# An attention-and-FFN kernel whose work order is written out, with the fourth pair's queries and keys issued ahead of four loads of values

## The chip, the cores and the metric

The kernel runs on one core of a Trainium2 chip. A core has five instruction streams: TensorE (PE, matrix multiplies into eight banks of PSUM), VectorE (DVE), ScalarE (ACT), GpSimd (POOL) and SyncE (SP). Each takes its instructions strictly in the order in which the program gave them to it. Data moves between HBM and the core's own memory (SBUF) by DMA; an engine issues a DMA as one more instruction of its stream. The metric is the device time of one execution in microseconds (us), median over the runs shown.

## The reference

The work is one block of attention and one gated feed-forward network. `q`, `k` and `v` are float32 of shape (8 batches, 8 heads, 576 positions, 64). For each of the 64 heads two attentions are added:

```python
q_d = q.reshape(B, H, Sd, 4, D).mean(axis=3)      # k_d, v_d alike; Sd = 144
out_d = softmax(scale * q_d @ k_d.T) @ v_d        # 144 x 144 scores
out_up = np.repeat(out_d, 4, axis=2)
mask = np.abs(pos[:, None] - pos[None, :]) < 4    # a band of 7 positions
out_local = softmax(where(mask, scale * q @ k.T, -1e9)) @ v
attn_out = out_up + out_local                     # (8, 8, 576, 64)
x = attn_out.transpose(0, 2, 1, 3).reshape(4608, 512)
out = (np.maximum(x @ w_gate, 0) * (x @ w_val)) @ w_out
```

`w_gate` and `w_val` are 512 x 1536, `w_out` is 1536 x 512, the output is 4608 x 512, all float32. The kernel computes in float16 and accumulates in float32.

## The kernel before, in words

**Tiling.** Heads are worked in pairs, 32 of them: pair p holds two heads of batch p // 4. The four pairs of a batch give the 512 columns of x for that batch's 576 tokens, pair kk of the batch giving the 128 columns of group kk (tile `xT`). The feed-forward network then runs on these tokens: for each of twelve blocks of 128 hidden columns a gate product and a value product (4 matmuls each, one for each kk), a ReLU on ACT, a product on DVE; after that the second product `y` with `w_out`, a copy on ACT and a store.

**Names.** An operation is named by its kind and its pair or its tokens. For pair p:

- `lq`, `lk` load queries and keys (SP, L1430); `lv0` to `lv3` load values in pieces (SP, L1674 and L1680; lv0 is an edge piece of two DMAs). SP keeps eight loads in flight: each waits for the landing of the one eight before.
- `cast` turns q and k into float16 (L1329 on ACT, L1330 on DVE or POOL), `T` transposes them on PE and sums the pooled groups (L1456, L1460), `ev0` and `ev1` copy the transposed halves out of PSUM, `pl` the pooled ones (both L1329/L1330).
- `Sl` and `Sd` are the local and the pooled scores on PE (L1518, L1530); for later pairs they stand together as `S`. `mx`, `sub`, `exp`, `sm`, `rc`, `nrm` are the local softmax: maximum (DVE, L1573), subtraction (L1576), exponential (ACT, L1589), sum (DVE, L1611), reciprocal (DVE, L1613), product (L1615). `dmx`, `nb`, `exd0..2`, `rcd`, `nrd` are the pooled one: maximum (DVE, L1592), its negative (POOL, L1595), exponentials (ACT, L1605), reciprocal (DVE, L1627), product (L1631).
- `tr0`, `tr1` transpose the local weights on DVE (L1621), `W` the pooled ones on PE, and `evw` copies the latter out.
- `vc` casts the values to float16 (`vw`), `VP` pools them on PE (L1695), `vd` copies that out (`vdz`).
- `V` multiplies weights with values on PE (L1731, L1739), `od` copies one half of its result on ACT (L1750), and `xa0`, `xa1` add the other half to it on DVE and write `xT` (L1759).
- `hg` and `hv` are the gate and value products of the feed-forward network (PE, L1798), `rl` the ReLU (ACT, L1812), `gm` the product (DVE, L1819). `hg0_0` is hidden block 0 of the first 512 tokens. Only for the blocks 0 and 1 the products are split: the part `a` takes the columns of pairs 0 to 2 and the part `b` those of pair 3. `hg512_0` and `hg512_6` take the last 64 tokens of the batch, six hidden blocks at once.
- `wg`, `wv` load three hidden blocks of the first weights each (POOL's DMA queue, L1380), `wo` the second ones.

**Stages.** The first four pairs are the *head* of the program: their q and k are loaded in another form (48 partitions, into the tile `gT`) and nothing of the feed-forward network can run until three pairs are done. From then on, attention of the next batch is worked between the products of the current one.

**What sets the order.** The kernel builds a graph of 1771 operations, each with its engine or a choice of engines, a length, a priority and what it depends on. A planner, `list_schedule` (L1071), simulates the five engines, the DMA engines and the fetch of instructions, and always takes the operation that can start first; ties go by priority. The tables `RANKS`, `SHIFT` and `ASK` move single operations in this. The planner also picks the engine of an operation that has a choice (`alts`), the PSUM banks, and how many matmuls on zeros PE runs in a gap ahead of an operation (`fill`, L1360). Operations are then emitted in the planned order of their starts, and that order is what each engine's stream holds:

```python
order = list_schedule(ops, {"F": [0, 1, 2, 3], "A": [4, 5, 6, 7]},
                      {PE: 0.05, ACT: 0.05, DVE: 0.05, POOL: 0.05, SP: 0.05})
```

The planner's numbers act on the order alone; at run time an engine starts an instruction when the one before it is done and what it waits for has arrived.

## Time and profile before

| | before |
|---|---|
| median of 3 runs | 362.51 us |
| lowest and highest | 362.36 and 363.07 us |
| profiled execution, device time | 361.35 us |
| its span, first to last instruction | 359.6 us |
| granted TensorE clock in it | 0.999 |

The profiled execution is 1.16 us (0.3%) under the median, so differences that are read from it are worked against 361.35 us and carried to the median afterwards. 1.75 us of it lie around the span.

The views used below are these. The *page* gives the busy time of each engine and the chain of work that ended last, by engine. The *windows view* gives one row for each stretch of time: the stretch and its length; for PE, weight loads (PEld), DVE, ACT and POOL the busy time with the number of instructions; the granted clock; the share of the DMA engines; GB/s. The *timeline* lists instructions by their start: start, length, engine, line, operation, output<-inputs, shape, and in brackets the idle time of the engine ahead of it with what ended it. The *groups view* puts instructions with one line, engine, operation and shape together: count, then busy us and the mean ns of one, then the idle time ahead of them. The *view of DMA issues* gives for one group of transfers its KB each and the median us from issue to landing.

### The profile page before, as it was taken

Reading aid. Unit: us, or ns where it says so; the run is one execution under the profiler, and the core shown is the slowest. Engines: PE = TensorE matmul, PEld = TensorE weight load, DVE = VectorE, ACT = ScalarE, POOL = GpSimd, SP = SyncE. Lnnn points to the kernel's source line nnn. Section 1 sums busy time; section 2 is a strip of 40 time slices with the busy share of each in tenths; the row PEclk is TensorE's granted clock in tenths of the full one; section 3 lists DMA queues with packets and bytes.
Section 4 is the critical chain, followed back from the end, with each engine's and each line's share of the span. In section 5 each row is a group of like instructions: output and inputs, shape, how many; then the busy total and the mean of one; then the engine's idle time right before and its main releaser. Section 6 shows DMA issues by size and latency. Waiting matters only on the chain.

```text
span 359.6 us, 10503 instructions
## 1 busy us (share of the span) xinstructions
PE 350.2 (97%) x4241; PEld 182.5 (51%) x4241; DVE 247.9 (69%) x477; ACT 202.8 (56%) x481; POOL 204.5 (57%) x240
## 2 busy tenths in 40 slices
...
GB/s 190 201 272 255 195 227 292 110 185 152 259 232 212 228 280 167 278 224 264 198 230 233 190 271 182 215 261 224 217 237 65 47 93 26 0 60 59 0 75 102
DMA packets 122067, 64.80 MB, mean 180 GB/s; under 512 B 100386, under 2 KB 106402, under 8 KB 122018
## 3 DMA queue, kind: packets, MB, share of 16 engines
...
q0 software_dynamic: 5824, 4.72, 8.6%
...
## 4 chain that ended last, share of the span: by engine, by line
PE 90%; POOL 5%; DMA 1%; issue 1%; DVE 1%; ACT 1%; POOLq 0%; SPq 0%
PE bank L1798 52%; PE bank L1864 25%; PE bank L1518 4%; PE bank L1731 2%; PE bank L1739 2%; DMA gT<-in_q_dram 1%; PE bank L1530 1%; POOL wo_sb L1330 1%; PE bank L1640 1%; PE bank L1695 1%; POOL vw L1352 1%; POOL wd L1631 1%; PE bank L1843 1%; POOL vw L1330 1%; POOL e L1615 1%
## 5 line engine op out<-in xcount | busy, mean ns | idle before, releaser
L1819 DVE TENSOR_TENSOR gT<-r,bank 128x512 f16<-128x512 f16 (+1 forms) x112 | 74.6, 666 | 64.1 <-PE bank L1798 59.9
L1798 PE MATMUL bank<-xT,wg_sb 128*128 128x512 f16 (+2 forms) x528 | 112.2, 341 | 0.0
L1798 PE MATMUL bank<-xT,wv_sb 128*128 128x512 f16 (+2 forms) x528 | 112.2, 341 | 0.0
L1812 ACT ACTIVATE r<-bank 128x512 f16<-128x512 f32 (+1 forms) x112 | 65.1, 583 | 67.2 <-PE bank L1798 62.9
L1864 PE MATMUL bank<-wo_sb,gT 128*128 128x512 f16 x420 | 96.6, 379 | 0.0
L1798 PEld LDWEIGHTS <-wg_sb 128*128 128x128 f16 x528 | 44.2, 98 | 45.5 <-issue 0.4
L1798 PEld LDWEIGHTS <-wv_sb 128*128 128x128 f16 x528 | 44.2, 98 | 44.6 <-issue 0.6
L1864 PEld LDWEIGHTS <-gT 128*128 128x128 f16 x420 | 39.8, 98 | 44.6 <-issue 0.4
L1873 ACT COPY y_sb<-bank 128x512 f32<-128x512 f32 x35 | 20.5, 586 | 52.0 <-PE bank L1864 49.6
L1330 POOL CAST vw<-vw 128x1536 f16<-128x1536 f32 x28 | 40.9, 1461 | 2.7 <-DMA vw<-in_v_dram 1.9
L1507 DVE TENSOR_REDUCE qkd<-qkT 128x288 f16<-128x1152 f16 x28 | 37.5, 1340 | 3.7 <-ACT qkT L1329 3.5
L1586 POOL TENSOR_TENSOR s_sb<-s_sb,mx 128x384 f32<-128x384 f32 x28 | 23.2, 831 | 28.8 <-DVE mx L1583 27.9
L1605 ACT ACTIVATE wd<-bank,nmb 128x144 f16<-128x144 f32 x96 | 35.6, 381 | 4.3 <-POOL nmb L1595 3.1
L1621 DVE STREAM_TRANSPOSE at<-e 64x384 f16<-64x384 f16 x64 | 36.4, 569 | 1.6 <-POOL e L1615 0.9
L1615 POOL TENSOR_TENSOR e<-e,rs 128x384 f16<-128x384 f16 x32 | 26.8, 839 | 14.7 <-DVE rs L1613 11.3
L1631 POOL TENSOR_TENSOR wd<-wd,rsd 128x432 f16<-128x432 f16 x32 | 29.0, 908 | 8.7 <-DVE rsd L1627 6.8
L1759 DVE TENSOR_TENSOR xT<-bank,od_sb 128x288 f16<-128x288 f32 (+2 forms) x68 | 26.7, 430 | 9.9 <-ACT od_sb L1750 9.8
L1717 POOL TENSOR_TENSOR vs<-v 104x512 f32<-104x512 f32 x20 | 25.3, 1267 | 2.1 <-DMA v<-in_v_dram 1.9
L1329 ACT COPY qkT<-tq 128x1152 f16<-128x1152 f16 x21 | 25.3, 1205 | 1.5 <-DMA tq<-c 1.4
L1518 PEld LDWEIGHTS <-qkT 64*32 64x32 f16 x1536 | 17.2, 90 | 11.9 <-issue 7.3
L1518 PE MATMUL bank<-qkT 64*32 64x32 f16 x1536 | 20.6, 180 | 1.0 <-DVE xT L1759 0.7
L1330 POOL CAST c<-qk 128x1152 f16<-128x1152 f32 x16 | 18.2, 1147 | 5.3 <-issue 3.9
...
## 6 DMA issues: line engine op xcount, KB each, us to landing
vw<-in_v_dram SPq DMA_DIRECT2D x126, 96.0 KB, 4.7
...
wv_sb<-in_moe_w_val_dram POOLq DMA_DIRECT2D x4, 384.0 KB, 10.0
wg_sb<-in_moe_w_gate_dram POOLq DMA_DIRECT2D x4, 384.0 KB, 9.4
wo_sb<-in_moe_w_out_dram POOLq DMA_DIRECT2D x4, 384.0 KB, 8.3
```

The costliest lines, as they stand in the source:

```text
L1330: return lambda o: engine[eng].tensor_copy(out=dst, in_=src(o))
L1507: nc.vector.tensor_reduce(out=qkd[S3].rearrange("p (x t) -> p x t", x=2), in_=qk_sums, axis=AX.X, op=ALU.add)
L1518: nc.tensor.matmul(out=scv[32 * c : 32 * c + 32, i, :], lhsT=cols(hh, q0 + step * 24 * blk, 32), rhs=cols(hh, k0 + step * (24 * blk - 3), 32),
L1605: exd.append(add(ACT, 0.37, lambda o, i=i: nc.scalar.activation(out=_sap(wd_, 0, 128, 256 * i + K0, kd_cols), in_=_sap(dview()[:, i, :], 0 ...
L1615: r["nrm"] = nrm = add_any(either(lambda o, e: e.tensor_tensor(out=e_, in0=e_, in1=bc12(rs[S3]), op=ALU.mult), (POOL, 0.84), (DVE, 0.5)), ...
L1621: tr.append(add(DVE, 0.575, lambda o, lo=lo: nc.vector.transpose(out=at2[S3][lo : lo + 64, :, lo // 2 : lo // 2 + 32], in_=e_[lo : lo + 64 ...
L1631: r["nrd"] = nrd = add_any(either(lambda o, e: e.tensor_tensor(out=_sap(wd_, 0, 128, K0, w3), in0=_sap(wd_, 0, 128, K0, w3), in1=_sap(rsd[ ...
L1759: nc.vector.tensor_tensor(out=xT[:, kk, (c1 + lo) % XR : (c1 + lo) % XR + hi - lo].rearrange("p (t f) -> p t f", f=4), in0=bank[V.banks[hf ...
L1798: nc.tensor.matmul(out=bank[(h or o).banks[0]][:, n * x : n * x + n], lhsT=w_sb[:, kk, bass.ts(jj, 128)], rhs=xT[:, kk, x_col(t0) : x_col( ...
L1812: rl = add(ACT, 0.17 + 0.00083 * n * m, lambda o: nc.scalar.activation(out=rt[:, 0 : n * m], in_=bank[f1.banks[0]][:, 0 : n * m], func=AF. ...
L1819: gm = add(DVE, 0.15 + 0.00104 * n * m, lambda o: nc.vector.tensor_tensor(out=gT[:, js[0] : js[0] + m, pos : pos + n], in0=rt[:, 0 : n * m ...
L1864: nc.tensor.matmul(out=bank[parts[0].banks[0]], lhsT=gT[:, jj, col : col + 128], rhs=wo_sb[:, jj, :], start=(jj == 0), stop=(jj == NJJ - 1))
```

## The change

The planner, its tables and its models of DMA and instruction fetch (about 1100 lines) are taken out. In their place stands `ORDER`, a list of all 1771 operations by name. A word is a name with, where needed, the engine's letter (`:A`, `:D`, `:P`), the PSUM banks (`.03`) and the number of zero matmuls ahead of it with their bank (`+5@1`). A loop emits the operations word by word. The operations, their shapes and their arithmetic are the same. In after's text every line number is about 998 lower, so that L1330 is L332, L1430 is L432, L1680 is L682.

The order differs in the head and a little behind it; from about `hv0_4` on PE, `gm0_4` on DVE, the first load of `w_out` on POOL and `lv2_3` on SP each stream is the same as before. The places are three.

**SP, loads 13 to 20 of its stream** (`vw320`, `vw321`, `vw322` are the float32 values of pairs 0, 1, 2; `gT_76` takes the queries and keys of pair 3). Before:

```order
L1680 DMA vw321_65<-in_v_dram 32x12x64 x3
L1680 DMA vw320_64<-in_v_dram 32x12x64
L1674 DMA vw320_64<-in_v_dram 29x64
L1680 DMA vw320_64<-in_v_dram 32x11x64
L1680 DMA vw320_64<-in_v_dram 32x12x64
L1430 DMA gT_76<-in_q_dram 48x2x768
L1680 DMA vw322_66<-in_v_dram 32x12x64
L1430 DMA gT_76<-in_k_dram 48x2x768
```

After:

```order
L682 DMA vw321_65<-in_v_dram 32x12x64 x3
L432 DMA gT_76<-in_q_dram 48x2x768
L432 DMA gT_76<-in_k_dram 48x2x768
L682 DMA vw320_64<-in_v_dram 32x12x64
L676 DMA vw320_64<-in_v_dram 29x64
L682 DMA vw320_64<-in_v_dram 32x11x64
L682 DMA vw320_64<-in_v_dram 32x12x64
L682 DMA vw322_66<-in_v_dram 32x12x64 x2
```

The query and key loads of pair 3 (lq3, lk3) now stand ahead of four loads of values (five DMAs): lv2_0, lv0_0, lv1_0 of pair 0 and lv3_2 of pair 2.

**DVE, from the first local maximum on** (the tiles end on the slot of the pair; `e160`, `e161` are the local weights of pairs 0 and 1, `vw161` the float16 values of pair 1, `qkT2` q and k of pair 2). Before:

```order
L1573 TENSOR_REDUCE mx1_118<-bank0_138 128x12
L1576 TENSOR_TENSOR s_sb1_91<-bank0_138,mx1_118 128x384
L1592 TENSOR_REDUCE nmx1_127<-bank1_139 128x3
L1611 TENSOR_REDUCE sm0_120<-e160_92 128x12
L1613 RECIPROCAL rs0_123<-sm0_120 128x12
L1611 TENSOR_REDUCE sm1_121<-e161_93 128x12
L1613 RECIPROCAL rs1_124<-sm1_121 128x12
L1621 STREAM_TRANSPOSE at20_87<-e160_92 64x12x32 x2
L1627 RECIPROCAL rsd1_136<-smd1_133 128x6
L1621 STREAM_TRANSPOSE at21_88<-e161_93 64x12x32 x2
L1627 RECIPROCAL rsd0_135<-smd0_132 128x6
L1573 TENSOR_REDUCE mx2_119<-bank1_139 128x12
```

After:

```order
L575 TENSOR_REDUCE mx1_118<-bank0_138 128x12
L578 TENSOR_TENSOR s_sb1_91<-bank0_138,mx1_118 128x384
L332 CAST vw161_85<-vw321_65 128x1536
L578 TENSOR_TENSOR s_sb0_90<-bank7_145,mx0_117 128x384
L332 COPY qkT2_116<-bank3_141 128x96x6
L332 COPY qkT2_116<-bank2_140 128x96x6
L613 TENSOR_REDUCE sm1_121<-e161_93 128x12
L615 RECIPROCAL rs1_124<-sm1_121 128x12
L629 RECIPROCAL rsd1_136<-smd1_133 128x6
L613 TENSOR_REDUCE sm0_120<-e160_92 128x12
L594 TENSOR_REDUCE nmx2_128<-bank0_138 128x3
L575 TENSOR_REDUCE mx2_119<-bank1_139 128x12
```

The cast of pair 1's values (vc1, on POOL before) and the two copies of pair 2 (ev0_2, ev1_2, on ACT before) stand in DVE's stream now. Further down it, up to the last `xT` piece of pair 2, come the normalizing products of pairs 1 and 3 (nrm1, nrm3), the copy of pair 0's pooled weights (evw0) and the pooled values of pairs 1 and 2 (vd1, vd2), and behind that vd3, ev1_5 and cast6; one transpose of pair 3 (tr1_3) moves behind that piece. In turn pl0 and pl1 go from DVE to ACT. cast2 and cast3 go from POOL to ACT, vc3 to ACT, cast1 to DVE, cast4 and cast7 to POOL.

**POOL, from its first cast on** (`wg_sb`, `wv_sb` are the first weights). Before:

```order
L1330 CAST wo_sb_70<-gT_76 96x2x12x64 x3
L1380 DMA wv_sb_69<-in_moe_w_val_dram 128x4x384
L1380 DMA wg_sb_68<-in_moe_w_gate_dram 128x4x384
L1595 ISA
L1595 TENSOR_SCALAR nmb0_129<-nmx0_126 128x3
L1595 TENSOR_SCALAR nmb1_130<-nmx1_127 128x3
L1615 TENSOR_TENSOR e160_92<-e160_92,rs0_123 128x384
L1615 TENSOR_TENSOR e161_93<-e161_93,rs1_124 128x384
L1330 CAST vw160_84<-vw320_64 128x1536
L1330 CAST vw161_85<-vw321_65 128x1536
L1330 CAST wo_sb_70<-gT_76 96x2x12x64
L1595 TENSOR_SCALAR nmb2_131<-nmx2_128 128x3
```

After:

```order
L332 CAST wo_sb_70<-gT_76 96x2x12x64
L597 ISA
L597 TENSOR_SCALAR nmb0_129<-nmx0_126 128x3
L597 TENSOR_SCALAR nmb1_130<-nmx1_127 128x3
L332 CAST vw160_84<-vw320_64 128x1536
L382 DMA wv_sb_69<-in_moe_w_val_dram 128x4x384
L597 TENSOR_SCALAR nmb2_131<-nmx2_128 128x3
L633 TENSOR_TENSOR wd0_99<-wd0_99,rsd0_135 128x6x3x24
L617 TENSOR_TENSOR e160_92<-e160_92,rs0_123 128x384
L633 TENSOR_TENSOR wd1_100<-wd1_100,rsd1_136 128x6x3x24
L382 DMA wg_sb_68<-in_moe_w_gate_dram 128x4x384
```

The first loads of the weights (wv0, wg0) stand behind the cast of pair 0's values (vc0) and behind three normalizing products now; before, they stood ahead of all softmax work.

On PE the order around the head is new as well: VP1 before VP0, T3 behind VP0, VP3 ahead of `hg0_0a`, V3 right behind `hg0_0a` and T5, and S5 and T6 later among the first products; there are 46 zero matmuls ahead of operations instead of 41 (11 ahead of T2 instead of 3, 6 ahead of W0 instead of none).

The diff, cut to its core:

```diff
-class Fetch:
...
-class Dma:
...
-def list_schedule(ops, bank_pools, eps):
...
+ORDER = """
+zero3 zero8 lq0 zero5 zero7 pewarm.0 lk0 zero10 ld_id zero12 zero22 zero21 zero23 lk1 zero15 zero9
+lv3_0 zero11 zero13 lq1 zero14 zero16 lv2_2 zero17 zero18 lk2 zero19 cast0:P ld_mask ld_sums lv0_1
+lq2 T0.456+5@1 lv2_1 ev0_0:A lv1_1 cast1:D pl0:A ev1_0:A lv3_1 T1.123+5@0 lq3 lk3 ev1_1:A Sl0.7
+pl1:A ev0_1:A Sd0.4 lv2_0 lv0_0 warm Sl1.0 dmx0 lv1_0 mx0 lv3_2 Sd1.1 nb0 cast2:A lv0_2 dmx1 lv2_3
+mx1 nb1 sub1 exd0_1 lv1_2 vc1:D exd1_1 T2.230+11@2 exd2_1 lv1_3 sub0 exd0_0 exp1 ev1_2:D exd1_0
+lv3_3 ev0_2:D pl2:A exd2_0 vc0:P sm1 exp0 Sl2.1+2@1 cast3:A rc1 lq4 rcd1 Sd2.0 sm0 wv0 VP1.2 lk4
+dmx2 VP0.5 mx2 nb2 T3.674+1@3 vd0:A rcd0 sub2 nrd0:P rc0 ev1_3:A nrm1:D exp2 nrm0:P lv0_3 ev0_3:A
+sm2 exd0_2 tr1_1 nrd1:P W0.5+6@1 pl3:A tr0_0 exd1_2 lq6 Sl3.4+2@1 wg0 tr1_0 exd2_2 lk6 rc2 rcd2
+mx3 nrm2:P Sd3.6+2@1 evw0:D nrd2:P dmx3 V0.75 vd1:D nb3 sub3 vc2:P exd0_3 W1.3+1@0 exp3 W2.1+1@0
+exd1_3 sm3 evw1:A tr1_2 VP2.2+3@0 exd2_3 tr0_1 od0 evw2:A vd2:D xa0_0 V1.03+4@0 lv3_5 rcd3 tr0_2
+nrd3:P lv2_5 vc3:A rc3 lv0_5 V2.12 xa1_0 nrm3:D W3.4 wg1 od1 lv1_5 od2 VP3.6+1@5 xa0_1 evw3:A wv1
+xa0_2 cast5:A xa1_1 xa1_2 cast4:P lv2_4 tr0_3 hg0_0a.0+1@5 vd3:D T5.57 tr1_3 wg2 lv0_4 V3.46+1@1
+ev0_5:D wv2 hv0_0a.3 ev1_5:D od3 wg3 xa0_3 hg0_1a.1 xa1_3 wv3 hv0_1a.2 pl5 lv1_4 T4.57 lv3_4
+hg0_0b hv0_0b cast6:D hg0_1b rl0_0 hv0_1b S5.46 ev0_4:A gm0_0 hg0_2.0 ev1_4:A msk5 rl0_1 lv0_6
+dmx5 T6.57 rl0_2 gm0_1 hv0_2.1 nb5 zerov exd0_5 mx5 lv1_6 ev1_6:A hg0_3.3 gm0_2 ev0_6:A pl4
+hv0_3.2 rl0_3 sub5:P lv3_6 hg512_0.0 vc5:P gm0_3 hv512_0.1 rl512_0 pl6 lv0_7 exd1_5 S4.57 exd2_5
...
+"""
...
-        return add(eng, dur, lambda o: engine[eng].memset(ap, 0.0), prio=prio, name="zero",
+        return add(eng, dur, lambda o: engine[eng].memset(ap, 0.0), prio=prio, name=f"zero{len(ops)}",
...
-    for o in ops:
-        o.prio += SHIFT.get(o.name, 0.0)
-        o.after = ASK.get(o.name, o.after)
-    order = list_schedule(ops, {"F": [0, 1, 2, 3], "A": [4, 5, 6, 7]},
-                          {PE: 0.05, ACT: 0.05, DVE: 0.05, POOL: 0.05, SP: 0.05})
-    owners = [o for o in order if o.banks]
+    named = {o.name: o for o in ops}
+    engines = {e[0]: e for e in (ACT, DVE, POOL)}
     with tc.manual_schedule():
-        last = 0.0
-        for o in order:
-            if o.eng == PE:
...
+        for word in ORDER.split():
+            word, _, fill = word.partition("+")
+            word, _, banks = word.partition(".")
+            name, _, eng = word.partition(":")
+            o = named.pop(name)
+            o.banks = [int(b) for b in banks]
+            emit = next(f for e, _, f in o.alts if not eng or e == engines[eng])
+            if fill:
+                n, _, b = fill.partition("@")
+                emit_zeros(int(b), int(n))
+            emit(o)
+    assert not named, "an operation is in no list"
```

1225 lines of the change are left out of this document (118 added, 1107 removed).

## The prediction

> **What bounds the kernel now.** First the page: how busy each engine is, and which engine the chain of work that ended last runs through.
>
> ```profile
> span 359.6 us, 10503 instructions
> PE 350.2 (97%) x4241; PEld 182.5 (51%) x4241; DVE 247.9 (69%) x477; ACT 202.8 (56%) x481; POOL 204.5 (57%) x240
> PE 90%; POOL 5%; DMA 1%; issue 1%; DVE 1%; ACT 1%; POOLq 0%; SPq 0%
> ```
>
> PE sets the time, and only 9.4 us of the span are without PE work. Where these lie, the windows view tells: first two stretches of the head, then three further on.
>
> ```profile
> core 0: us, PE busy (x) PEld busy (x) DVE busy (x) ACT busy (x) POOL busy (x), PEclk, DMA share, GB/s
> 0.00:12.20 12.20, 10.14 (x135) 5.31 (x135) 4.72 (x12) 3.86 (x6) 8.01 (x15) 1.00 0.87 198
> 12.20:32.10 19.90, 16.58 (x351) 9.98 (x348) 16.02 (x38) 12.80 (x43) 18.23 (x21) 1.00 1.18 254
> 32.30:45.60 13.30, 12.47 (x250) 7.74 (x248) 10.16 (x15) 10.49 (x18) 8.79 (x11) 1.00 1.30 199
> 45.60:60.00 14.40, 14.40 (x266) 8.48 (x263) 13.13 (x28) 12.31 (x36) 8.44 (x13) 1.00 1.14 260
> 60.00:120.00 60.00, 59.92 (x785) 31.14 (x778) 42.99 (x85) 37.11 (x88) 38.19 (x43) 1.00 1.00 197
> ```
>
> From 45.6 us on PE is full (14.40 of 14.40, 59.92 of 60.00), and its order from there is unchanged. So a delay or a gain that PE has at 45.6 us reaches the end whole. Before 32 us PE's busy time tells little, since zero matmuls fill its gaps; there the dates count. PE's timeline has the marks:
>
> ```profile
> 22.21 0.69 PE L1456 MATMUL bank<-ident_sb,wo_sb 96*128 96x96 f16 x12 [0.26 <-POOL wo_sb L1330]
> 25.57 0.53 PE L1518 MATMUL bank<-qkT 64*32 64x32 f16 x48
> 32.38 0.81 PE L1798 MATMUL bank<-xT,wg_sb 128*128 128x512 f16 x3
> 33.77 0.40 PE L1695 MATMUL bank<-vw,sums_sb 128*32 128x256 f16 x6
> 37.79 0.20 PE L1518 MATMUL bank<-qkT 64*32 64x32 f16 x4 [0.66 <-DVE xT L1759]
> 38.15 0.24 PE L1530 MATMUL bank<-qkd 64*32 64x144 f16 x4 [0.17 <-DVE xT L1759]
> 45.63 0.60 PE L1798 MATMUL bank<-xT,wg_sb 128*128 128x512 f16 x2
> ```
>
> They are T3 (22.21, freed by POOL's cast of pair 3), Sl3 (25.57), the first product hg0_0a (32.38), VP3 (33.77), S5 (37.79, after a hole of 0.66) and hg0_4 (45.63). DVE's timeline has what hg0_0a needs, the last pieces of `xT` for pairs 0 to 2:
>
> ```profile
> 31.27 0.82 DVE L1759 TENSOR_TENSOR xT<-bank,od_sb 128x288 f16<-128x288 f32 x2
> ```
>
> It ends at 32.09 and hg0_0a starts 0.29 later. So the head is a chain through DVE: 38 instructions from 12.20, 16.02 us busy in 19.90.
>
> **DVE's list up to hg0_0a.** The groups view of DVE in that stretch lists all 38:
>
> ```profile
> L1621 DVE STREAM_TRANSPOSE at<-e 64x384 f16<-64x384 f16 x8 | 4.5, 566 | 0.7 <-POOL e L1615 0.6
> L1592 DVE TENSOR_REDUCE nmx<-bank 128x3 f32<-128x432 f32 x4 | 2.4, 596 | 0.0
> L1759 DVE TENSOR_TENSOR xT<-bank,od_sb 128x288 f16<-128x288 f32 x6 | 2.4, 434 | 0.0
> L1576 DVE TENSOR_TENSOR s_sb<-bank,mx 128x384 f32<-128x384 f32 x4 | 2.2, 557 | 0.1
> L1573 DVE TENSOR_REDUCE mx<-bank 128x12 f32<-128x384 f32 x4 | 2.2, 545 | 1.3 <-PE bank L1518 1.3
> L1611 DVE TENSOR_REDUCE sm<-e 128x12 f32<-128x384 f16 x4 | 2.1, 535 | 0.2
> L1613 DVE RECIPROCAL rs<-sm 128x12 f32<-128x12 f32 x4 | 0.9, 228 | 0.1
> L1627 DVE RECIPROCAL rsd<-smd 128x6 f32<-128x6 f32 x4 | 0.8, 192 | 1.7 <-ACT wd L1605 1.7
> ```
>
> Their sum is 17.5 us; 16.02 busy means that each overlaps the next by 0.04. The 3.9 idle us are waits for scores (1.3), ACT's pooled exponentials (1.7) and POOL's products (0.7). The change takes tr1_3 out (0.57) and puts eight in, which stand nowhere in this stretch. The nearest rows are from the groups of the whole run:
>
> ```profile
> L1330 DVE CAST qkd<-bank 128x288 f16<-128x288 f32 x2 | 0.9, 458 | 5.7 <-PE bank L1460 5.7
> L1330 DVE COPY qkT<-bank 128x640 f16<-128x640 f16 x1 | 0.8, 826 | 2.0 <-PE bank L1456 2.0
> L1330 DVE COPY qkT<-tq 128x1152 f16<-128x1152 f16 x1 | 0.6, 587 | 0.0
> L1352 DVE MEMSET vw<- 128x1536 f32 x2 | 2.7, 1338 | 0.5 <-issue 0.5
> L1329 ACT CAST qkd<-bank 128x288 f16<-128x288 f32 x2 | 0.8, 423 | 0.0
> ```
>
> - vc1, a cast of 128x1536 float32: scaled from the 1152-element copy 0.587 x 1536/1152 = 0.78, from the memset of 1536 words 1.34. I take 0.90, nearer to the copy, which also reads and writes.
> - ev0_2, ev1_2, evw0, copies of 576 from PSUM: 0.826 x 576/640 = 0.74 each, 2.22 together.
> - nrm1, nrm3: the subtraction's 0.557 each, 1.11.
> - vd1, vd2, casts of 256 from PSUM: 0.458 x 256/288 = 0.41 each, 0.82.
>
> Sum 5.05, less 8 x 0.04 is 4.73; less 0.53 for tr1_3 the list comes to 16.02 + 4.73 - 0.53 = 20.2 us without any idle time, more than the old 19.90 with it. So even a list without a single hole ends later than the old one, unless it starts sooner.
>
> It starts at 12.0 instead of 12.2: T1 waits for cast1, which on DVE is shorter by about half a us (0.90 like vc1, on POOL 1.46 by a row below), but Sl0 then waits for ev1_0 behind pl0 on ACT (423 ns by the last row), so I keep 0.2 of it (bounds 0 and 0.3). What idle time remains is 0.6 where a sum stands right behind the exponential that it needs (exp3 and sm3; 0.52 for an exponential, by a row below), and 0.3 for mx3 (further down). Then the last `xT` piece ends at 12.0 + 20.2 + 0.9 = 33.1, and hg0_0a starts at **33.2, 0.8 later**. From both sides: vc1 at 0.78, a start at 11.9 and holes of 0.4 give 32.5; vc1 at 1.34 and holes of 1.5 give 34.2.
>
> [...]
>
> **The moved loads, T3 and mx3.** Rows for the transfers (the view of DMA issues, at 9.33, 12.44 and 14.86 us) and for POOL:
>
> ```profile
> vw<-in_v_dram SPq DMA_DIRECT2D x1, 96.0 KB, 4.7
> gT<-in_q_dram SPq DMA_DIRECT2D x1, 288.0 KB, 4.9
> wg_sb<-in_moe_w_gate_dram POOLq DMA_DIRECT2D x1, 384.0 KB, 8.8
> 12.44 0.59 SPq L1430 DMA_DIRECT2D gT<-in_q_dram  x1
> 14.85 0.75 POOL L1380 DMA_DIRECT2D wg_sb<-in_moe_w_gate_dram  x1
> 17.88 2.87 POOL L1330 CAST vw<-vw 128x1536 f16<-128x1536 f32 x2
> 20.70 1.46 POOL L1330 CAST wo_sb<-gT 96x1536 f16<-96x1536 f32 x1
> 20.84 0.52 ACT L1589 ACTIVATE e<-s_sb 128x384 f16<-128x384 f32 x1 [0.65 <-DVE s_sb L1576]
> 22.33 0.90 POOL L1631 TENSOR_TENSOR wd<-wd,rsd 128x432 f16<-128x432 f16 x1
> 23.20 0.82 POOL L1615 TENSOR_TENSOR e<-e,rs 128x384 f16<-128x384 f16 x1
> ```
>
> q and k of pair 3 gain: cast3 leaves POOL's line, where it stood behind two casts of values until 20.70, and runs on ACT behind exp0. DVE's rows up to sub0 put exp0 at 16.3, so cast3 is done at 18.3 if it takes POOL's 1.46. But on PE T3 now stands behind VP0, which needs vc0 and so the delayed values. Before, the last load for pair 0 lands between 14.0 (9.33 + 4.7) and 17.3 (12.44 + 4.9), say 15.7. Now 2 x 288 KB, 590 kB, go ahead: 2.3 us at 254 GB/s, 3.0 at 198. So the values are there at 18.0 to 18.7, vc0 (half of 2.87) at 19.5 to 20.2, T3 at 19.9 to 20.6: some 1.6 to 2.3 sooner than 22.21. From T3 to the end of Sl3 it was 3.9 us (25.57 + 0.53 - 22.21), so mx3 may run from 23.8 to 24.5. DVE's 23 instructions ahead of mx3 come to 11.7 us by the rows above, so DVE is there at 23.7 without a hole and at 24.2 with the usual half. The fourth pair's gain is thus not cashed: DVE is not free sooner, and 0.3 us of wait is what I charge. With the values one us later still, nearly a whole us is lost.
>
> **From hg0_0a to hg0_4** PE took 45.63 - 32.38 = 13.25. VP3 has moved ahead (-0.33, from 33.77 to the next start). The two holes of 0.66 and 0.17 at S5 waited for `xT` of pair 3; S5 now stands behind all products that need it, so -0.83. New waits: T6 needs the bank that ev1_4 frees, and ev1_4 stands behind rl0_0 on ACT, 0.3; V3 needs tr1_3, now behind `xT`, 0.2 (bounds 0 and 1 for both). That is 12.6, and hg0_4 starts at 45.8, **0.2 later**.
>
> **Behind it.** tr1_3 (0.57), vd3 (0.41), ev1_5 (0.74, like ev1_2) and cast6 (0.59, the copy of 1152) are new for DVE in 32.3 to 45.6, 2.3 us in 13.30 - 10.16 = 3.1 idle ones, with the next stretch at 13.13 of 14.40. The softmax of pairs 4 to 6 is then somewhat late for PE: I take 0.3, bounds 0 and 1.
>
> Sum: 0.17 + 0.3 = 0.47 on 361.35, which is 361.8 for such an execution; on the median, 362.51 + 0.47 = **363.0 us**. About 0.2% (0.72 us, as much as the three runs lie apart) is what a measurement tells from no change. What costs nothing: ACT gives away ev0_2, ev1_2, evw0, vd1, vd2 and takes cast2, cast3, vc3, some 1.3 us more (3 x 1.46 against 2.22 + 0.82), with 7.1 of its 19.90 us idle to cover it; if that cover is gone, exp2 and exp3 come 1.3 later, and DVE's sums with them. The five further zero matmuls stand in gaps that end with a semaphore.
>
> **Rivals.**
>
> *The fourth pair pays (faster).* The list has no more holes than 0.4 (hg0_0a at 32.5 to 32.6), PE's 1.16 us behind it are won in full, with no new wait and no late softmax: +0.2 - 1.16 = -0.9, 361.6 us. For it: 3.0 of the 3.9 idle us were waits for scores and for exponentials, and in the new list other work stands in these places. Against it: 20.2 us of work have to go without a stop, and DVE's next two stretches have 4.4 idle us in 27.7.
>
> *Values too late (slower).* vc0 is what VP0, T3 and all of pair 3 stand behind. If each value piece waits out a whole landing of the larger loads (4.9), the last is there at 20.6, T3 comes at 22.5 and mx3 at 26.4, so DVE waits for 2.2 instead of 0.3: +0.47 + 1.9, 364.9 us. It decides from a landing of about 18.7 on. Against it: the first weights no longer share the queues with them.
>
> *Weights too late (slower).* wg0 was issued at 14.85. Now it stands behind nb2, nrd0, nrm0 and nrd1; DVE reaches rcd0 at about 20.3, the three products take 0.90 + 0.82 + 0.90, so it goes at 23.0 and lands at 31.8 by its 8.8, with hg0_0a at 33.2. If wv0's 384 KB still lie ahead at half of 254 GB/s, it is 3.1 later, 34.9: +1.7, 364.7 us.
>
> *DVE and POOL in each other's way (slower).* nrm1 and nrm3 have both operands in SBUF, which none of DVE's two-operand rows above has (each reads a bank), and POOL runs nrd0, nrm0 and nrd1 at that time. If one waits for the other, 0.9 for nrm1 and about as much for nrm3 at worst: +0.9 to 1.8, 364.3 us. [...]
>
> **Chances.** Forecast 0.46, its own range 362.2 to 363.8: same 0.28, slower 0.18. Fourth pair pays 0.34: faster 0.23, same 0.11. Values late 0.08, weights late 0.06, the two engines 0.06, all slower. Together faster 0.23, same 0.39, slower 0.38. The range takes in most of the faster and of the slower cases, 361.2 to 364.7.
>
> **What would show it.** DVE nearly without idle time from 12.0 to 33, vc1 at 0.9, hg0_0a near 33.2: the list. T3 near 20.2 with mx3 waiting little: the moved loads. No hole ahead of S5, hg0_4 at 45.8: PE's order. PE still full afterwards. Wrong it would be with hg0_0a before 32.6, with vc0 after 19, with wg0 as what hg0_0a waits for, with an idle DVE ahead of nrm1, or with new holes of PE between 46 and 60 us.

## The result, and the profile after

| | before | after |
|---|---|---|
| median | 362.36 us (7 runs) | 364.60 us (7 runs) |
| lowest and highest | 361.32 and 363.07 | 363.70 and 365.23 |
| ratio, after to before | | 1.0066, 95% interval 1.0047 to 1.0084 |
| profiled execution, its span | 361.35, 359.6 | 365.19, 363.4 |

The changed kernel is slower by 2.2 us (0.66%, clear of no change). The forecast was 363.0 us, no change that can be told. The profiled execution of before lies 1.0 us under its median of 362.36 and that of after 0.6 over its own, so the two traces are 3.8 us apart where the medians are 2.2 apart. In the whole document four executions count as a slower state and are left out of every ratio (368.82 of e5, 369.55 of e8, 594.18 of e11, 510.73 of before); without them the medians of e5, e8 and e11 are 364.3, 365.6 and 362.0.

The page of after:

```profile
span 363.4 us, 10501 instructions
PE 352.6 (97%) x4246; PEld 184.0 (51%) x4246; DVE 254.9 (70%) x487; ACT 201.8 (56%) x477; POOL 196.8 (54%) x234
PE 89%; DVE 5%; DMA 3%; ACT 1%; issue 1%; POOL 0%; SPq 0%; POOLq 0%; DVEq 0%
```

PE still sets the time, but 5% of the chain that ended last now runs through DVE and 3% through transfers, where it was 1% and 1%; the 5% through POOL are gone. The windows view of after, same stretches as before:

```profile
12.20:32.10 19.90, 16.05 (x313) 9.82 (x314) 17.18 (x34) 12.92 (x39) 9.69 (x13) 0.91 1.08 250
32.30:45.60 13.30, 13.19 (x185) 7.51 (x184) 13.10 (x27) 8.22 (x16) 8.98 (x11) 1.00 1.18 188
45.60:60.00 14.40, 14.18 (x300) 9.04 (x298) 13.60 (x25) 11.12 (x31) 8.98 (x12) 1.00 1.18 277
60.00:120.00 60.00, 59.59 (x815) 31.02 (x814) 43.33 (x85) 36.14 (x87) 36.98 (x42) 1.00 1.00 191
```

POOL's busy time in the head fell from 18.23 to 9.69, DVE's rose, and DVE has 13.10 of 13.30 us from 32.3 on. PE is no longer full behind 45.6 us. Its timeline dates the loss, hg0_0a first, then hg0_4:

```profile
35.20 1.01 PE L800 MATMUL bank<-xT,wg_sb 128*128 128x512 f16 x3
...
48.18 1.04 PE L800 MATMUL bank<-xT,wg_sb 128*128 128x512 f16 x4
```

hg0_0a came 2.82 us later than in before's trace (32.38), hg0_4 2.55 us (45.63). What held it in this execution stands in DVE's and POOL's timelines:

```profile
19.32 0.55 DVE L613 TENSOR_REDUCE sm<-e 128x12 f32<-128x384 f16 x1 [1.17 <-ACT e L591]
...
21.50 2.70 DVE L617 TENSOR_TENSOR e<-e,rs 128x384 f16<-128x384 f16 x1
24.12 0.54 DVE L613 TENSOR_REDUCE sm<-e 128x12 f32<-128x384 f16 x1
```

```profile
21.20 0.93 POOL L633 TENSOR_TENSOR wd<-wd,rsd 128x432 f16<-128x432 f16 x1
22.07 0.84 POOL L617 TENSOR_TENSOR e<-e,rs 128x384 f16<-128x384 f16 x1
22.86 0.92 POOL L633 TENSOR_TENSOR wd<-wd,rsd 128x432 f16<-128x432 f16 x1
23.71 0.82 POOL L382 DMA_DIRECT2D wg_sb<-in_moe_w_gate_dram  x1
```

nrm1 took 2.70 us on DVE, from shortly behind nrd0's start to 0.4 behind nrd1's end. The 1.17 us ahead of sm0 are a wait for exp0, which stands on ACT behind pl2, and pl2 reads T2. Inside T2 PE stood still with nothing but its issue named:

```profile
17.74 0.33 PE L462 MATMUL bank<-ident_sb,wo_sb 96*128 96x96 f16 x4 [1.53 <-issue]
```

A second look at the same kernel (below) shows nrm1 at 0.49, with hg0_0a at 34.35 waiting for a weight. So there are two causes at hg0_0a, and one hides the other.

### The profile page after: what moved, and what is told of

Same layout as the page of the kernel before. It is cut to its first block, busy times and chain, and to the rows that moved or that the text cites. A ratio compares the mean times of both kernels' runs of the same rounds, so it can differ in the third digit from the quotient of the medians.

```text
span 363.4 us, 10501 instructions
## 1 busy us (share of the span) xinstructions
PE 352.6 (97%) x4246; PEld 184.0 (51%) x4246; DVE 254.9 (70%) x487; ACT 201.8 (56%) x477; POOL 196.8 (54%) x234
## 4 chain that ended last, share of the span: by engine, by line
PE 89%; DVE 5%; DMA 3%; ACT 1%; issue 1%; POOL 0%; SPq 0%; POOLq 0%; DVEq 0%
PE bank L800 51%; PE bank L866 25%; PE bank L520 4%; PE bank L733 3%; PE bank L741 2%; DMA gT<-in_q_dram 1%; DMA gT<-in_k_dram 1%; DMA vw<-in_v_dram 1%; DVE at L623 1%; DVE e L617 1%; PE bank L532 1%; PE bank L697 1%; PE bank L642 1%; DVE vw L354 1%; PE bank L845 1%; DVE xT L761 1%
## 5 line engine op out<-in xcount | busy, mean ns | idle before, releaser
L332 POOL CAST vw<-vw 128x1536 f16<-128x1536 f32 x26 | 38.0, 1462 | 7.7 <-DMA vw<-in_v_dram 4.6
L588 POOL TENSOR_TENSOR s_sb<-s_sb,mx 128x384 f32<-128x384 f32 x28 | 23.2, 831 | 22.4 <-DVE mx L585 20.6
L617 POOL TENSOR_TENSOR e<-e,rs 128x384 f16<-128x384 f16 x30 | 25.2, 840 | 17.5 <-DVE rs L615 12.5
L594 DVE TENSOR_REDUCE nmx<-bank 128x3 f32<-128x432 f32 x32 | 18.9, 593 | 3.8 <-PE bank L532 3.7
```

What stands on the lines that cost most here:

```text
L332: return lambda o: engine[eng].tensor_copy(out=dst, in_=src(o))
L617: r["nrm"] = nrm = add_any(either(lambda o, e: e.tensor_tensor(out=e_, in0=e_, in1=bc12(rs[S3]), op=ALU.mult), (POOL, 0.84), (DVE, 0.5)), ...
```

## The experiments

Each kernel below is the kernel before or the changed one with a few words of the written order altered; the order of before was written out in the same form for this. All compute the whole reference. Line numbers differ by a few from kernel to kernel. Medians are over 6 to 12 runs beside 22 to 30 of before on the same chip. The dates of hg0_0a and hg0_4 are those of one profiled execution, whose time stands beside the median, and the last column is the idle time of PE from S4 on in it (gaps over 0.12 us, added up from the trace; in the new order S4 stands right ahead of hg0_4). Dates of single executions scatter: T1 came between 9.7 and 10.4 in the kernels with after's head, and between 10.2 and 11.1 in those with before's.

| kernel | median | profiled | ratio to before (95%) | hg0_0a | hg0_4 | PE idle from S4 on |
|---|---|---|---|---|---|---|
| before | 362.4 to 362.6 | 361.35 | | 32.38 | 45.63 | 0.00 |
| after | 364.60 | 365.19 | 1.0066 (1.0047 to 1.0084) | 35.20 | 48.18 | 1.42 |
| e12 after, second look | (1 run) | 363.92 | | 34.35 | 46.72 | 1.66 |
| e1 after, nrm1 on POOL | 366.09 | 365.52 | 1.0111 (1.0079 to 1.0142) | 35.36 | 49.55 | 0.67 |
| e2 after, 3 zero matmuls at T2 | 364.30 | 365.47 | 1.0051 (1.0029 to 1.0074) | 34.82 | 46.77 | 2.29 |
| e5 after, weights early | 364.72 | 363.68 | 1.0046 (1.0024 to 1.0067) | 33.62 | 46.78 | 1.55 |
| e6 after, weights early and 3 zeros | 363.01 | 362.73 | 1.0019 (1.0000 to 1.0038) | 32.50 | 45.54 | 1.21 |
| e10 e6 with exp2 ahead | 363.82 | 362.12 | 1.0025 (1.0005 to 1.0045) | 31.89 | 44.94 | 1.36 |
| e7 after, q and k back | 364.85 | 365.41 | 1.0063 (1.0044 to 1.0083) | 34.36 | 47.56 | 2.52 |
| e8 e6, q and k back | 365.84 | 363.72 | 1.0117 (1.0082 to 1.0152) | 34.75 | 47.34 | 0.59 |
| e13 e2 with lq6, lk6 late | 365.73 | 363.08 | 1.0077 (1.0039 to 1.0114) | 33.53 | 46.38 | 0.76 |
| e17 after, 6 zeros at T2 | 364.06 | 364.74 | 1.0045 (1.0024 to 1.0066) | 34.79 | 47.38 | 1.00 |
| e3 before, q and k ahead | 363.08 | 363.15 | 1.0015 (0.9990 to 1.0040) | 34.23 | 47.48 | 0.00 |
| e4 before, nrm1 on DVE | 362.20 | 362.52 | 0.9992 (0.9972 to 1.0013) | 33.03 | 46.29 | 0.60 |
| e9 before, weights late | 363.73 | 364.08 | 1.0044 (1.0022 to 1.0067) | 35.30 | 48.33 | 0.00 |
| e11 before's head, after's products | 362.06 | 594.18 | 0.9996 (0.9970 to 1.0022) | | | |
| e15 the same kernel again | 362.44 | 362.91 | 0.9985 (0.9963 to 1.0006) | 33.66 | 46.69 | 0.50 |
| e16 e15 with vc1 on DVE | 362.67 | 362.42 | 1.0018 (0.9992 to 1.0043) | 32.63 | 45.66 | 0.70 |
| e14 before, 11 zeros at T2, 2 at Sl2 | 362.61 | 362.73 | 1.0006 (0.9985 to 1.0027) | 32.63 | 45.88 | 0.90 |
| e18 before, 8 zeros at T2 | 362.89 | 363.59 | 1.0004 (0.9978 to 1.0029) | 32.01 | 45.27 | 1.94 |

One thing on record differs between these kernels besides the order: the granted clock of PE. In the traces one stretch of 3.4 us at 0.50 makes the mean of an execution about 0.995 (after, e7, e9), and one of 6.8 us makes it 0.991 (e8, e17). Before has 0.995 or less in 19 of its 129 executions beside the experiments, e15 and e18 in none of 12; but after has it in 3 of 7, the kernels with 3 or 6 zero matmuls ahead of T2 (e2, e6, e8, e10, e13, e17) in 52 of 59, and e9 in all 12. In some kernels these are the longer executions (after: 365.15 to 365.23 against 363.70 to 364.60; e10, below), in others not (e2, e6). So a part of what is put down to an order below may go through the clock, and no run separates the two.

### Is it nrm1, the stall in T2, or the moved loads?

e1:

```diff
-ev1_3:A nrm1:D exp2
+ev1_3:A nrm1:P exp2
```

> The changed kernel with one word altered: nrm1 goes back from DVE to POOL, between nrd0 and nrm0. Theory (DVE and POOL in each other's way): nrm1 took 2.70 us on DVE, 21.50 to 24.20, because POOL ran nrd0, nrm0 and nrd1 without a break from 21.20 to 23.77; without it sm2 starts near 21.6 instead of 24.12, POOL ends nrd1 0.84 later, hg0_0a comes at 33.3 to 34.0 instead of 35.20, and the time falls by 1.2 to 2.0, to about 363.0. Rival (the late sm0 behind T2's stall is the cause, and 2.70 only shows a wait that would be elsewhere): gain under 0.5 us, 364.1 or more. Rival (2.70 is nrm1's own length on DVE, whatever POOL does): the same gain as the theory's; the run of the kernel before with nrm1 alone on DVE tells these two apart.

e2:

```diff
-T2.230+11@2
+T2.230+3@2
```

> The changed kernel with 3 zero matmuls ahead of T2 instead of 11, as many as before. Theory (PE's own issue): T2 stood still for 1.53 us, from 16.2 to 17.74, with no releaser but the issue, 11 zero matmuls and 12 of T2's behind each other; with 3 the stall is under 0.3, T2 ends near 16.4 as cast2 ends at 13.96, pl2 and exp0 come 1.5 earlier, sm0 at 18.0 instead of 19.32. nrm1 then starts near 20.3, ahead of POOL's products at 21.20, and keeps 0.56 if the lock goes by who is first: 1.5 to 2.5 us less, about 362.6. If nrm1 still ends with nrd1 at 23.8 to 24.2, the gain is under 0.4. Rival (T2 stands for another reason, cast or bank): T2 still ends after 17.5 and the time stays at 364.6.

(The lock in e2's expectation is the author's guess at why nrm1 took 2.70 us; the runs show only the lengths of nrm1.) In both the last `xT` piece of pair 2 came 2.1 to 2.3 us earlier (33.71 and 33.46 instead of 35.78), as both theories asked. But hg0_0a did not follow. The view of PE's waits for e1, and PE's timeline for e2:

```profile
PE bank L797 <- DMA wg_sb<-in_moe_w_gate_dram: 2.1, 1, 2.1
```

```profile
34.82 0.82 PE L797 MATMUL bank<-xT,wg_sb 128*128 128x512 f16 x3 [1.78 <-DMA wg_sb<-in_moe_w_gate_dram]
```

The gain of the head went into a wait for wg0, the rival of late weights. The time of e1 was above all expectations (366.09): behind that hole, and into the products, PE ran at a granted clock of 0.50, as the windows view of e1 shows (the last column but two is the granted clock):

```profile
33.30:35.30 2.00, 0.00 (x0) 0.00 (x0) 1.78 (x5) 0.85 (x1) 2.00 (x4) 0.98 1.34 233
35.30:36.30 1.00, 0.94 (x3) 0.40 (x4) 0.00 (x0) 0.00 (x0) 1.00 (x2) 0.50 1.26 199
36.30:37.30 1.00, 1.00 (x9) 0.73 (x8) 0.00 (x0) 0.00 (x0) 1.00 (x2) 0.50 1.31 199
37.30:38.30 1.00, 1.00 (x13) 0.72 (x12) 0.91 (x2) 0.00 (x0) 0.11 (x1) 0.50 1.29 198
```

e3 and e4 do one part alone in the order of before:

```diff
-lv2_0 cast1:P ev1_0:A lv0_0 lv1_0 lq3 T1.123+8@0 lv3_2 lk3 Sl0.7
+lq3 lk3 lv2_0 cast1:P ev1_0:A lv0_0 lv1_0 T1.123+8@0 lv3_2 Sl0.7
```

> The kernel before, its whole order, with only lq3 and lk3 moved ahead of lv2_0, lv0_0, lv1_0 and lv3_2. Theory (the moved loads alone cost a little): the values of pair 0 land 2 to 3 us later, near 18.5, vc0 starts there instead of 17.88, and vc1, cast3 and T3 slip with it by 0.6 to 0.9, as cast3 still stands behind them on POOL: 0.3 to 0.9 slower than before, about 362.9. Rival (the loads are what made the change slow): 1.5 us slower or more, over 363.8. Rival (the earlier loads help by themselves): faster, under 362.0.

```diff
-lq6 nrm1:P tr0_0
+lq6 nrm1:D tr0_0
```

> The kernel before, its whole order, with only nrm1 on DVE instead of POOL. Theory (DVE and POOL in each other's way): it can start at 16.8, while POOL runs nrm0 (to 17.13) and then vc0, vc1 and cast3 without a break; it takes 0.9 to 4 us, its end falls together with the end of one of POOL's instructions, and the time is 0.3 to 2 us more. Rival (it is slow on DVE by itself): 2.7 us again, with an end that falls together with nothing of POOL. Rival (no contention): 0.56 us as the subtraction of the same shape, and a time within 0.4 of before.

The load move in the title costs 0.5 us in the old lists by the medians (e3), and its interval reaches from 0.4 less to 1.5 more, so by itself it does not account for the 2.2 of the change. (In e3's trace vc0 came 1.46 later than in before's and hg0_0a 1.85 later; the medians show less than these two traces.) nrm1 alone on DVE is harmless where it met only one product of POOL (e4: 0.68 us), so 2.70 is not its own length.

### The weights, alone and with the rest

e9 moves only the weights in the order of before, wv0 behind vc0 and wg0 behind nrd1:

```diff
-lv1_3 wv0 sub1 ... T2.230+3@2 wg0 lq4 ... vc0:P ev1_2:A ... nrd1:P tr0_2
+lv1_3 sub1 ... T2.230+3@2 lq4 ... vc0:P wv0 ev1_2:A ... nrd1:P wg0 tr0_2
```

> The kernel before, its whole order, with only wv0 moved behind vc0 and wg0 behind nrd1 on POOL, as the change has them. It prices the late weights alone. Theory (weights are a chain of their own): wg0 goes at 24.9 and, with the 9.8 to 11.2 us that it took in the changed kernel and its variants, lands at 34.7 to 36.1, so hg0_0a starts there instead of 32.38 and the time is 1.5 to 3 us more, 364 to 365.5. Rival (the landing is hidden, as wg0 shares the queues with less then): under 363.0.

```profile
35.30 0.82 PE L797 MATMUL bank<-xT,wg_sb 128*128 128x512 f16 x3 [0.81 <-DMA wg_sb<-in_moe_w_gate_dram]
```

Alone they cost 1.1 us by the medians and 1.6 by the ratio (0.44%, 0.22 to 0.67), at the low end of the 1.5 to 3 that was expected. PE waits for the weight again, 0.81 us. The list is later too (last `xT` piece at 34.71): the two issues of 0.97 and 0.83 us now stand in POOL's line, wv0 ahead of vc1, and T3 took 2.00 us at a granted clock of 0.50, where it took 1.19 in before. So the price holds all three. e5 undoes this part in the changed kernel (wv0 and wg0 go from their places there to behind nb1); e6 has the second pair of lines as well:

```diff
-nb1 sub1
+nb1 wv0 wg0 sub1
...
-T2.230+11@2
+T2.230+3@2
```

> The changed kernel with wv0 and wg0 issued early again, behind nb1 and ahead of vc0 (at about 14 to 15.7 us instead of 19.99 and 23.71). Theory now (two chains end together in the changed kernel: DVE's, stretched by nrm1, lets hg0_0a run at 35.1, and wg0, which landed at 33.5 there and at 34.8 and 35.3 in the two variants with a faster DVE): wg0 lands before 26, but DVE still holds hg0_0a at about 35, and vc0 comes up to 0.8 later for sharing the queues, so nothing is won: 364.0 to 365.5. Rival (the weights alone made the change slow): 362.5 to 363.2.

> The changed kernel with both: weights early and 3 zero matmuls ahead of T2, with which nrm1 started at 20.16, ahead of POOL's products, and took 0.49. Theory (two chains): only now hg0_0a moves, to where the last xT piece was in the variant with 3 zero matmuls alone, 33.5 plus up to 0.8 for later values, and no wait of PE for a weight is left; time 362.3 to 363.3, 1.3 to 2.3 under the changed kernel, about that of the kernel before. Rival (there is a third bound, or PE's clock, or the products behind hg0_0a): over 363.8.

Both times came out as the theory of two chains said. e5 is at 364.72; its ratio lies 0.2% under that of the changed kernel, with intervals that overlap. e6 is at 363.01, 1.6 us less than the changed kernel, and there the intervals are apart; it is also the 363.0 of the forecast. In e6 hg0_0a starts where before had it (32.50), and its last matmuls wait for DVE's `xT` again, not for a weight:

```profile
33.23 0.74 PE L797 MATMUL bank<-xT,wg_sb 128*128 128x512 f16 x2 [0.35 <-DVE xT L758]
```

What holds DVE in e5 is not nrm1, as expected, but a third chain. Its timeline:

```profile
20.66 0.49 DVE L614 TENSOR_TENSOR e<-e,rs 128x384 f16<-128x384 f16 x1
23.15 0.55 DVE L610 TENSOR_REDUCE sm<-e 128x12 f32<-128x384 f16 x1 [2.00 <-ACT e L588]
```

sm2 waits 2.00 us for exp2, which stands on ACT behind ev1_3, and so behind T3, VP0, vc0 and the values, which landed at 19.07 in that execution. e10 takes exp2 out of that line:

```diff
-vd0:A rcd0 sub2 nrd0:P rc0 ev1_3:A nrm1:D exp2
+exp2 vd0:A rcd0 sub2 nrd0:P rc0 ev1_3:A nrm1:D
```

> The changed kernel with early weights, 3 zero matmuls ahead of T2, and exp2 moved ahead of vd0 and ev1_3 on ACT. In the variant with early weights alone sm2 waited for exp2 from 21.16 to 23.15, exp2 standing behind ev1_3, T3, VP0, vc0 and the late values of pair 0. Theory (the values are the third chain): exp2 runs at 21 right behind sub2 whatever the values do, sm2 starts by 21.9, and the time is 0 to 0.8 less than 363.0 of the variant without it. Rival (sm2 is not what holds the list): no difference, or slower as vd0 and T3's copies come later.

```profile
20.35 0.88 DVE L614 TENSOR_TENSOR e<-e,rs 128x384 f16<-128x384 f16 x1
21.16 0.54 DVE L610 TENSOR_REDUCE sm<-e 128x12 f32<-128x384 f16 x1
```

The wait is gone and hg0_4 is the earliest of all kernels (44.94, 0.7 ahead of before). The median did not follow: 363.82, a miss. The trace cannot say why, since it is of an execution of 362.12 us. That one and one of 361.80 had a granted clock of 0.999 or more; the ten others, at 0.991 to 0.995, took 363.03 to 365.07.

### Undoing the move in the title

e7 puts SP's order of before into the changed kernel, e8 into e6:

```diff
-lq3 lk3 ev1_1:A ... lv2_0 lv0_0 warm Sl1.0 dmx0 lv1_0 mx0 lv3_2
+ev1_1:A ... lv2_0 lv0_0 warm Sl1.0 dmx0 lv1_0 lq3 mx0 lv3_2 lk3
```

> The changed kernel with SP's order of before: lq3 and lk3 behind the values of pair 0. It asks what the move in the title is worth within the new lists. Theory: values land 2 us sooner, vc0 near 17 instead of 18.58, wv0 and wg0 go sooner by 0.5 to 1.5; cast3 waits for lk3 until near 19 to 20, T3 near 21 instead of 20.70. nrm1 still meets POOL's products. Within 0.7 of the changed kernel either way, 363.9 to 365.3. Rival (the move is what costs): 363.2 or less. Rival (the move pays): 365.5 or more.

> The changed kernel with weights early, 3 zero matmuls ahead of T2, and SP's order of before; what remains of the change are the new lists of DVE, ACT, POOL and PE. Theory: values land near 16.5 as before, vc0 starts at 17 to 17.9, T3 hangs on cast3 and lk3 (near 20 then) at 21 to 22; DVE's list is full anyway, so within 0.5 of the variant with the two edits alone, about 362.5. Rival (earlier values free POOL and PE, and the new lists then pay): under 361.8.

e7 agrees, 364.85. e8 misses by 3 us (365.84 where 362.5 was expected). DVE's waits in e8 say where:

```profile
DVE sm L610 <- ACT e L588: 3.0, 2, 2.4
```

Values came sooner (vc0 at 16.86), but lk3 later, so that T3 ran at 21.48 instead of 19.99 (e6) and took 2.10 us instead of 1.18, at a granted clock of 0.50. ev1_3 came late with it, and exp2 behind ev1_3 made sm2 wait 2.4 us. Whichever of the two loads goes second, exp2 stands behind it. Beside early weights the new lists lose without the early q and k; beside late weights (e7) and in the old lists (e3) it makes no difference that can be told. How much of e8's loss is the clock's is not shown: all six of its executions had 0.995 or less.

### The second look, and what lies behind the head

> The changed kernel once more, unaltered, for a second look at its trace. It tells which of the waits seen belong to the order and which to one execution: nrm1 at 2.70 us (the theory of POOL's unbroken products: again over 0.9 whenever it starts behind nrd0), the stall of 1.53 in T2 (in two variants with the same 11 zero matmuls T2 took 1.34 and 1.37, so probably not again), hg0_0a at about 35 with wg0 landing between 33 and 35.5.

The timelines of DVE, POOL and PE in the second execution of the changed kernel:

```profile
20.39 0.49 DVE L614 TENSOR_TENSOR e<-e,rs 128x384 f16<-128x384 f16 x1
22.55 0.55 DVE L610 TENSOR_REDUCE sm<-e 128x12 f32<-128x384 f16 x1 [1.66 <-ACT e L588]
```

```profile
23.74 0.82 POOL L379 DMA_DIRECT2D wg_sb<-in_moe_w_gate_dram  x1
```

```profile
34.35 0.82 PE L797 MATMUL bank<-xT,wg_sb 128*128 128x512 f16 x3 [1.16 <-DMA wg_sb<-in_moe_w_gate_dram]
...
46.60 0.19 PE L517 MATMUL bank<-qkT 64*32 64x32 f16 x2 [0.24 <-issue]
...
62.20 0.29 PE L517 MATMUL bank<-qkT 64*32 64x32 f16 x19 [0.99 <-issue]
...
136.22 1.02 PE L797 MATMUL bank<-xT,wg_sb 128*128 128x512 f16 x4 [0.43 <-issue]
```

Here sm0 was sooner, nrm1 started at 20.39, ahead of nrd0 (21.23 in both), and was done in 0.49; T2 lost 0.5 us to PE's issue instead of 1.53. hg0_0a waits for wg0, which took 10.6 us from issue to landing by the view of DMA issues, 9.8 in the first look:

```profile
wg_sb<-in_moe_w_gate_dram POOLq DMA_DIRECT2D x1, 384.0 KB, 10.6
```

```profile
wg_sb<-in_moe_w_gate_dram POOLq DMA_DIRECT2D x1, 384.0 KB, 9.8
```

The last three rows of PE are a part of the loss that no chain of the head explains: in S4, S7 and hg1152_5 it stands still with nothing but its issue named, 1.66 us in all, and at the same three instructions in the first look (0.22, 0.41 and 0.79, the last put down to an exponential on ACT there). In before's trace there is none. But that is one execution: with the same instructions on PE e4 has 0.60 in S7, and e3 and e9 have none. e17 and e18 ask whether the count of instructions ahead does it (the change has 10 more rows on PE):

```diff
-T2.230+11@2
+T2.230+6@2
```

> The changed kernel with 6 zero matmuls ahead of T2 instead of 11, so that PE's stream has as many instructions as before (8484 rows instead of 8494) and every instruction behind hv0_4 has its old place in it. Theory (a stall of PE's issue belongs to a place in the stream): no hole in S4 and hg1152_5, at most 0.6 in S7 (one run with the old places had that), under 0.7 us in all behind hg0_4 instead of 1.42 and 1.66; time 363.0 to 363.9 instead of 364.6. Rival (the stalls come from what the head leaves behind): holes at the same three instructions, over 1 us, and 364.4 or more.

```diff
-T2.230+3@2
+T2.230+8@2
```

> The kernel before with 8 zero matmuls ahead of T2 instead of 3, so that its PE stream has 8494 rows as the changed kernel's. Theory: holes in S4, S7 or hg1152_5, 0.6 to 1.7 us in all, where before has none, and a time of 363.0 to 364.2 instead of 362.5, although the head is as before. Rival (the number of rows does not matter): no such hole, 362.2 to 362.8.

In e17 S4 and hg1152_5 are clean and S7 has 0.42, as expected; a wait of another kind (0.58 at V23, for a transposing transfer) stands beside it. The time fell by 0.5 us only, to 364.06, just above the range; but the head of e17 was slow for another reason, T3 taking 2.13 us at a granted clock of 0.50, so the time does not price the stalls. In e18 a hole of 0.98 came up in S7, but none in the other two (0.97 more are waits for transposing transfers), and the time did not move clearly (362.89). So the count moves these stalls about; that it makes them, and what they cost in the median, is not shown. e14 changes the place of the zero matmuls at an unchanged count:

```diff
-T2.230+3@2 ... Sl2.1+10@5
+T2.230+11@2 ... Sl2.1+2@5
```

> The kernel before with 11 zero matmuls ahead of T2 and 2 ahead of Sl2, instead of 3 and 10. Theory (the number is harmless by itself): within 0.4 of before, as T2 ends by 17 and Sl2 waits until 18.17 anyway. Rival (PE's issue pays for it): T2 stalls, ends after 17.2, and 0.7 us more or worse.

It is harmless, 362.61. Why 3 instead of 11 gave about 1.0 us beside early weights (0.27% between the ratios of e6 and e5) stays open: T2 ended 0.8 us sooner there, but the values also landed sooner, for a reason that the traces don't show.

e13 tried what wg0 waits behind, by issuing lq6 and lk6 behind lv3_4 (in e2):

```diff
-exd1_2 lq6 Sl3.4+2@1 wg0 tr1_0 exd2_2 lk6 rc2 ... T4.57 lv3_4
+exd1_2 Sl3.4+2@1 wg0 tr1_0 exd2_2 rc2 ... T4.57 lv3_4 lq6 lk6
```

> The changed kernel with 3 zero matmuls ahead of T2 and with lq6 and lk6 (2 x 576 KB for pairs 6 and 7) issued 11 us later, behind lv3_4; the first weights stay late. Theory (wg0 is slow because these loads share the engines with it): wg0, issued near 23.6, lands in 7 to 9 us instead of 11.2, by 31 to 32.5, PE no longer waits for it, hg0_0a starts near 33.6 with DVE's list, and the time falls from 364.3 to about 363.0. Rival (its own packets set its pace): wg0 still lands after 34 and the time stays at 364.0 or more.

wg0 took 9.6 us and landed at 33.49, later than expected and sooner than in e2 (34.77). The time is a miss: 365.73 instead of 363.0, in executions from 362.94 to 367.97, of which the trace shows one of 363.08. What makes wg0 slow when it is issued late is not settled: issued before 16 us it took 8.3 to 9.2 us in eleven traces, issued behind 22 us 8.9 (e9) to 11.2 (e2) in eight.

### The products behind hg0_0a, and vc1

e11 and e15 are the same kernel, before's order up to hg0_0a and the changed order from there; the trace is read in e15. e16 has vc1 on DVE behind rc1 as well. Against the changed order from there, VP3 alone is elsewhere; the second pair of lines is e16's:

```diff
-VP3.6+1@5 wv1 ... hg0_0a.0+1@5 vd3:D T5.57
+wv1 ... hg0_0a.0+1@5 VP3.6 vd3:D T5.57
...
-rc1 ev0_2:A ... Sl2.1+10@5 tr1_1 exd2_0 vc1:P
+rc1 vc1:D ev0_2:A ... Sl2.1+10@5 tr1_1 exd2_0
```

> The kernel before up to hg0_0a, and the change's order from there (V3 right behind hg0_0a and T5, S5, T6 and S4 later, vd3, ev1_5 and cast6 on DVE, cast4 and cast7 on POOL); VP3 stays behind hg0_0a. It prices the second half of the change alone. Theory (the products' new order is worth what the forecast gave it): hg0_0a at 32.4 as before, no hole ahead of S5, hg0_0a to hg0_4 in 12.0 to 12.8 instead of 13.25; time 0.4 to 1.2 less than before, 361.3 to 362.1. Rival (the new waits at V3 and T6 and DVE's debt eat it): 362.5 or more.

> The kernel before up to hg0_0a and the change's order from there, once more, for an undisturbed trace. Theory: hg0_0a to hg0_4 in 12.0 to 12.8 instead of 13.25, no hole ahead of S5, median 361.8 to 362.3, 0.3 to 0.8 under before. Rival: 13.2 or more, no difference.

> The same, with vc1 on DVE right behind rc1 instead of on POOL. Theory: DVE takes it in 0.95 at about 16.8 to 17.8, where it had idle time, and POOL goes from vc0 to cast3 without 1.45 in between; cast3 then hangs on lk3 (near 20), T3 starts near 21.5 instead of 22.21, and the list to hg0_0a gets 0.3 to 0.7 shorter: 361.4 to 361.9. Rival (vc1 meets vc0 on POOL and one waits for the other, or lk3 is the bound): no gain or up to 0.5 slower.

The medians, 362.06 and 362.44, may be a little under before, but both intervals include no change. From hg0_0a to hg0_4 it takes 13.03 us, not 12.0 to 12.8: the holes at S5 are gone, but T5 and V3 stand ahead of hv0_0a now, and T5 waits for ACT's cast5:

```profile
35.39 0.68 PE L455 MATMUL bank<-ident_sb,c 128*128 128x128 f16 x9 [0.58 <-ACT c L328]
```

e16 gains nothing by vc1 on DVE. Its timeline of POOL and DVE shows them in each other's way once more:

```profile
17.00 2.33 POOL L614 TENSOR_TENSOR e<-e,rs 128x384 f16<-128x384 f16 x2 [0.20 <-DVE rs L612]
...
17.50 1.14 DVE L329 CAST vw<-vw 128x1536 f16<-128x1536 f32 x1
```

nrm0 and nrm1, 1.62 together in before, take 2.33, and vc1 1.14 instead of the 0.95 it had in the changed kernel. No version beats both kernels clearly.

## Why the prediction was wrong, by its own steps

**PE full behind 45.6 us: right for before's trace, not for the change.** A delay at hg0_4 did reach the end, but PE lost another 1.20 and 1.42 us behind it (and 0.22 and 0.24 in S4, right ahead of it), where the forecast had 0.3 for a late softmax. No late softmax shows there; the stalls are of PE's issue, but for 0.79 in the first look. Their cause stays open.

**DVE's list: right as a sum by luck, wrong in its waits.** The last `xT` piece was forecast at 33.1. It ended at 33.61 in the second look and at 35.78 in the first. In the second, DVE was busy 18.77 us between 11.98 and 33.61, not 20.2: vc1 measured 0.95 (0.90 forecast) and nrm1 0.49 (0.557), but evw0 0.44 (0.74). Idle time was 2.86, not 0.9, of which 1.66 is sm2 waiting for exp2. So 1.4 us too much work hid 2.0 us of missing waits. In the first look the same idle time (2.81) met a nrm1 of 2.70, and the list alone was late by 2.7.

**The moved loads: the dates were right, the place of the wait was not.** Values landed at 18.43 and 18.46 (forecast 18.0 to 18.7), T3 ran at 20.70 and 20.68 (19.9 to 20.6, so 0.1 past it). But what was late was not mx3. It was sm2: exp2 stands behind ev1_3 on ACT, and so behind T3. I had looked at who reads T3's results, not at who is queued behind that reader.

**Late weights: this is the step that failed, together with the waits of DVE's list.** The forecast took wg0's 8.8 us from a load issued at 14.85, put it at 23.0 and let it land at 31.8, 1.4 us ahead of hg0_0a, so it charged nothing. In the second look it went at 23.74 and took 10.6 us: landed 34.30, hg0_0a at 34.35, after 1.16 us of waiting. In the first look it landed at 33.48, and DVE's list held hg0_0a longer. e9 prices the late weights in the order of before (1.1 to 1.6 us), e1 and e2 show them standing behind DVE's chain, and e6 that the loss goes when both are undone. The rival of late weights had 0.06 and 364.7 us, and the kernel measured 364.60; that the two agree so closely is partly luck, as the rival had neither sm2's wait nor the stalls, and a landing at 34.9.

**DVE and POOL in each other's way: the effect is there, the price was too small and it does not always strike.** The sum charged nothing for it; the rival had 0.9 for nrm1, an estimate by the 0.90 of one POOL product; that one engine waits for the other was its supposition, shown by no row of before. When nrm1 started behind nrd0 it cost 2.21 (2.70 against 0.49) in one execution and 0.39 to 0.46 in four (e6, e7, e8, e10); when it started ahead of nrd0, nothing in three (e2, e5, the second look), 0.46 in e17 and 0.69 in e13. POOL's issue of wv0 overlapped nrm1 in e13, but also in e2 and the second look, where it cost nothing. In after nrm1 ended at 24.20, 0.4 behind the last of POOL's three products (nrd1, 23.78); in e16 it was nrm1 on POOL that took 1.54, beside vc1 on DVE; a nrm1 that came first took 0.49 in e2, e5 and the second look. Why one execution waits for one product and another for three was not shown, nor why nrm1 took 1.18 in e13, where no product of POOL had started before it.

**From hg0_0a to hg0_4: right in size.** 12.37 and 12.98 in two looks, forecast 12.6; e15 with 13.03 shows that part of the gain is eaten at T5.

The sum, for the second look: hg0_0a came 1.97 later (forecast 0.82), the stage behind it gave back 0.88 (0.65), and PE's stalls behind hg0_4 added 1.42 (0.3 was put for another reason). That is 2.5, and the span rose by 2.5. Both are counted from before's one trace, which has no stall and lies under its median, so how much of the 1.42 belongs to the change is not known.
